# An FFT filter ahead of an expert layer: where the second stage puts one product, and what ScalarE does in which order there

## The chip, the cores and the metric

One core of one Trainium2 chip runs the whole program. The metric is the device time of one execution in microseconds (us); less is better. Five engines work side by side, each through its own queue in order: TensorE (PE in the profile; PEld are its weight loads), VectorE (DVE), ScalarE (ACT), GpSimd (POOL) and SyncE (SP), which only issues transfers here. An instruction that has to wait for a semaphore holds back all that stands behind it on its engine.

## What is computed

```python
h_filt = (np.maximum(pos_emb @ w1, 0.0) @ w2) * np.exp(-0.01 * pos)[:, None]
u = x * v                                     # 2 x 12480 x 128
Uf = np.fft.rfft(u, n=2 * S, axis=1)
Hf = np.fft.rfft(h_filt, n=2 * S, axis=0)
y = np.fft.irfft(Uf * Hf[None], n=2 * S, axis=1)[:, :S]
a = (x * y).reshape(24960, 128)
h = a @ moe_w_in                              # 128 -> 2048
g = np.maximum(h, 0.0) + moe_alpha * np.minimum(h, 0.0)
out = g @ moe_w_out                           # 2048 -> 128
```

A long convolution by way of a Fourier transform, a gate with `x`, and a two-layer network for every token. The kernel does the transforms as matrix products with tables, and the two weight matrices arrive as 64-bit words, whose two 32-bit halves the kernel itself turns into fp32 numbers.

## The kernel before

The transform is split in stages, and the 128 channels in two groups of 64 (`NG = 2`). For each group, stage 1 transforms over one index, stage 2 over the other and multiplies by the filter's spectrum, and stage 3 goes back along one index; after that, stage 4 and the expert layer (phase B) take most of the span. In the trace stage 2 runs twice: the **first run** stands at about 136 to 240 us, the **second run** at about 363 to 459 us, with stage 3 of the first group and stage 1 of the second group between them.

Stage 2 (`stage2`) goes over 90 frequencies, two at a time: 45 **pairs**, numbered 0 to 44 here. `skew` writes the code as a pipeline by hand: in each step every stage works on a pair of its own, and the order in which the stages stand in the call is the order of the instructions. What one step holds, with the engine:

- `low` (POOL, line 936) of the pair three back: the rest that is lost in the cast to fp16, two reads of SBUF.
- `high` (ACT, line 932) of the pair two back: the product's cast to fp16 into `z`.
- `total` of the pair one back: `real` (POOL, line 914) and `imaginary` (DVE, line 919), the real and the imaginary sum of the complex product; both read two tiles of SBUF.
- `transform` of this pair: 24 matmuls (PE, lines 881 to 886) into one of three PSUM buffers `mm`, then `hidden` (ACT, line 897), which copies the filter's two spectra out of PSUM into `hs`, and `product` (DVE, line 909): two multiplications of 512 elements, PSUM by SBUF into SBUF; `ta` is the data times the filter's real part, `tb` the data times its imaginary part.
- `neg` (ACT, line 848) for the pair two ahead: the negated sines that its matmuls read.
- `more`: one piece of a list of other work, below.
- `load` (SP, line 841): a table of 512 KB for every second pair, six steps ahead of its matmuls.

The last two pairs' products are not in this pipeline but in `end`, whose pieces a planner (`Plan`) orders together with the next stage; it keeps `product`, `real` and `imaginary` as they are.

In the first run the list of `more` is `weights_in`: the first weight matrix in four blocks of 512 columns. `read(n)` takes a block's words from its load in seven pieces, one in each step: an absolute value (ACT, line 595, into the PSUM bank `mb[1]`), four bit operations (DVE, lines 561, 564, 567 and 570; the last completes the fp32 numbers, and behind it SP issues the load of the next block, line 586, into the tile that it has just read), a square (ACT, line 600) and four matmuls with one column each (PE, line 601) into columns 0 to 15 of the PSUM bank `mb[0]`. `later(read, 6)` starts a block every six steps. Then come two pieces for a power-of-two scale, and `halves(n)`, started every three steps: four scaled diagonals (ACT, line 605), one matmul that needs them (PE, line 606, into `mb[1]`), a multiplication (DVE, line 607, SBUF by PSUM), a cast, a subtraction (POOL, line 609) and a store (SP, line 610). In the second run the list is short: `unscale` does six small operations on DVE (lines 1141 to 1147, one partition), and two steps later four matmuls with one column each (`turn`, line 1151) into `mb[0]`.

Of the kernel before, what the change touches and what calls it, by code (L numbers as in the profile page):

```python
# [104 lines left out]
def skew(items, *stages):  # L105

    n = len(items)
    for t in range(n + max(j for j, _ in stages)):
        for j, stage in stages:
            if 0 <= t - j < n:  # L110
                stage(items[t - j])
# [178 lines left out]
def body(ctx, tc, A, out, stop=None, dbg=None):  # L290
# [278 lines left out]
    def completed(out, t, lo):  # L569
        ve.scalar_tensor_tensor(out=out, in0=lo, scalar=29, in1=t, op0=ALU.logical_shift_right, op1=ALU.bitwise_or)  # L570

    def weights_in(mb, ru, du, pu, su):

        w = units(ru, 2).bitcast(I32)
        lo, hi = (w.rearrange("p (n w) -> p w n", w=2)[:, j] for j in range(2))
        t = mb[1].bitcast(I32)
        d = [units(u) for u in du]
        sq = units(su).bitcast(BF16)
        diag = [units(ru).bitcast(BF16)[:, j * 512:(j + 1) * 512].rearrange("p (f c) -> p f c", c=128) for j in range(2)]

        def four(x):
            return x.rearrange("p (f c) -> p f c", c=128)

        def load(n):
            if n < NFT // 4:
                sy.dma_start(out=w, in_=A["wi"][:, n * 512:(n + 1) * 512].bitcast(I32))

        def bound():
            load(0)
            ve.tensor_tensor(out=room_a, in0=keep, in1=keep, op=ALU.mult)  # L590
            ve.tensor_single_scalar(out=room_a, in_=room_a, scalar=1.0, op=ALU.max)

        def read(n):
            x = sq[:, n % 2 * 512:n % 2 * 512 + 512]
            yield lambda: ac.activation(mb[1], hi.bitcast(F32), AF.Abs)
            yield lambda: within(ve, mb[1])
            yield lambda: shifted(t, t)
            yield lambda: signed(t, hi)
            yield lambda: (completed(d[n].bitcast(I32), t, lo), load(n + 1))
            yield lambda: ac.activation(x, d[n], AF.Square)  # L600
            yield lambda: [te.matmul(mb[0][:, 4 * n + f:4 * n + f + 1], four(x)[:, f], ones[:, :1], start=True, stop=True) for f in range(4)]

        def halves(n):
            p, g = half(units(pu[n % 2])), diag[n % 2]
            yield lambda: [ac.activation(g[:, f], eye, AF.Copy, scale=pw[:, 4 * n + f:4 * n + f + 1]) for f in range(4)]
            yield lambda: te.matmul(mb[1], ones, g.rearrange("p f c -> p (f c)"), start=True, stop=True)
            yield lambda: ve.tensor_tensor(out=d[n], in0=d[n], in1=mb[1], op=ALU.mult)
            yield lambda: ac.activation(p[:, :, 0], four(d[n]), AF.Copy)
            yield lambda: po.tensor_tensor(out=p[:, :, 1], in0=four(d[n]), in1=p[:, :, 0], op=ALU.subtract)
            yield lambda: sy.dma_start(out=w_d[n], in_=p)  # L610

        def later(gen, s):
            parts = [list(gen(n)) for n in range(NFT // 4)]
            for x in range(s * (NFT // 4 - 1) + len(parts[0])):
                fs = [parts[n][x - s * n] for n in range(NFT // 4) if 0 <= x - s * n < len(parts[n])]
                yield lambda fs=fs: [f() for f in fs]

        yield bound
        yield none
        yield from later(read, 6)  # L620
        yield lambda: (ve.tensor_tensor(out=mb[0][:, 16:32], in0=mb[0][:, :16], in1=room_a, op=ALU.mult),
                       scales(mb[0][:, 32:48], mb[0][:, 16:32], pw, 192))
        yield lambda: inverse(ipw, pw)
        yield from later(halves, 3)

    def load_words(raws, n):
        sy.dma_start(out=raws[n].bitcast(I32), in_=A["wo"][:, n * 512:(n + 1) * 512].bitcast(I32).rearrange("p (u e) -> p u e", u=2))
# [54 lines left out]
    def phase_a():  # L682
# [167 lines left out]
        def stage2(tu, au, bu, hu, nu, extra, loaded=0):  # L850

            st = {}
            tws = {}

            def load(f0):
                if f0 % FB == 0:
# [10 lines left out]
            def transform(f0):  # L867
# [19 lines left out]
                st["p", f0] = p, *(units(u[x % n]).rearrange("p (a m) -> p a m", a=2) for u, n in ((hu, 2), (au, 4), (bu, 2)))  # L887
                if f0 < NF - 4:
                    hidden(f0)
                    product(f0)  # L890

            def hidden(f0, b0=0, b1=NB):

# [11 lines left out]
            def product(f0, b0=0, b1=NB):  # L905
                p, hs, ta, tb = st["p", f0]
                m = slice(b0 * 2 * ZC, b1 * 2 * ZC)
                for t, a in ((ta, 0), (tb, 1)):
                    ve.tensor_tensor(out=t[:, :, m], in0=p[:, :, m], in1=hs[:, a:a + 1, m].to_broadcast([128, 2, (b1 - b0) * 2 * ZC]), op=ALU.mult)  # L909

            def real(f0, b0=0, b1=NB, e=po):
                _, _, ta, tb = st["p", f0]
                m = slice(b0 * 2 * ZC, b1 * 2 * ZC)
                e.tensor_tensor(out=ta[:, 0, m], in0=ta[:, 0, m], in1=tb[:, 1, m], op=ALU.subtract)  # L914
# [4 lines left out]
                ve.tensor_tensor(out=ta[:, 1, m], in0=ta[:, 1, m], in1=tb[:, 0, m], op=ALU.add)  # L919

            def total(f0):
                real(f0)
                imaginary(f0)

            def place(f0, b0, b1):

# [14 lines left out]
            def until(last, stage):  # L941
                return lambda f0: stage(f0) if f0 <= last else None

            skew(list(range(0, NF, 2)), (9, until(NF - 10, low)), (8, until(NF - 8, high)), (7, until(NF - 6, total)),
                 (6, until(NF - 4, transform)), (4, neg), (4, more), (0, load))

            def end(P):

# [502 lines left out]
```

## Time and profile before

| | us |
|---|---|
| median of 3 runs | 1632.72 (1629.75 to 1633.54) |
| profiled execution | 1629.31 |
| its span, first to last instruction | 1627.5 |
| PE busy | 1549.3 (95% of the span) |
| DVE, ACT, POOL busy | 1288.0, 1329.6, 1036.1 |
| PE's granted clock, mean | 0.985 of 2.4 GHz |

The profiled execution has 1.8 us around its span. A matmul's record is longer than its distance from the next one, since matmuls are pipelined, so PE's busy time says little of how close PE is to its limit; the distance from start to start does. The same holds for a VectorE instruction: its record overlaps that of the next by some 0.08 us. Most of the span, from about 500 us on, is phase B, which the change leaves as it is.

### The profile page before, as it was taken

How to read it: one execution, taken by the hardware profiler on the slowest of the kernel's cores; microseconds unless marked ns; L12 is line 12 of the kernel's file. 1: busy time of each engine (PE TensorE's matmuls, PEld its weight loads, DVE VectorE, ACT ScalarE, POOL GpSimd, SP SyncE). 2: the span in 40 equal slices, each digit the busy share in tenths (PEclk: the TensorE clock that was granted, in tenths of full speed). 3: DMA queues.
4: the chain of work that ended last, by engine and by line, in shares of the span. 5: the costliest groups of instructions: out<-in, count | busy, mean ns of one | idle time of the engine just before them, and what ended most of it. 6: DMA issues, size and time to landing. Idle time of an engine off the chain costs nothing.

```text
span 1627.5 us, 34281 instructions
## 1 busy us (share of the span) xinstructions
PE 1549.3 (95%) x13452; PEld 1090.9 (67%) x13452; DVE 1288.0 (79%) x1867; ACT 1329.6 (82%) x2203; POOL 1036.1 (64%) x728
## 2 busy tenths in 40 slices
PE   6888888999988999999999999999999999999998
PEld 4778878889987566666666666665666666666664
DVE  7998988989987777777777777778777777777775
ACT  6887777887866888888888888888888888888886
POOL 6797896978963655556655566555565555665554
PEclk8999998999999999999999999999999999999999
DMA  6453437874358320202212021120202202022000
GB/s 200 138 155 130 157 133 207 250 222 153 130 159 237 96 56 25 57 21 57 62 35 57 21 57 49 49 57 21 57 30 68 57 21 57 21 77 57 20 11 20
DMA packets 91663, 141.86 MB, mean 87 GB/s; under 512 B 7057, under 2 KB 59891, under 8 KB 90061
## 3 DMA queue, kind: packets, MB, share of 16 engines
q1 hardware_dynamic: 90525, 139.10, 29.3%
q8 instruction: 105, 1.72, 0.4%
q10 hardware_dynamic: 976, 0.57, 0.1%
q14 instruction: 57, 0.47, 0.1%
HBM read 99.02 MB, written 40.63 MB: 86 GB/s over the span
## 4 chain that ended last, share of the span: by engine, by line
PE 72%; DVE 13%; POOL 4%; ACT 4%; issue 4%; DMA 3%; SPq 0%; POOLq 0%; ACTq 0%; DVEq 0%
PE hp L1273 31%; PE o L1273 31%; DVE ring L909 6%; DVE ring L919 3%; POOL ring L761 2%; DMA first<-in_xv 1%; PE yp L280 1%; PE yp L281 1%; PE yp L282 1%; PE mm L1010 1%; PE mm L1012 1%; POOL ring L752 1%; PE mm L1011 1%; DVE z L810 1%; POOL ring L724 1%
## 5 line engine op out<-in xcount | busy, mean ns | idle before, releaser
L1350 POOL TENSOR_TENSOR g_lo<-ring,g_hi 128x780 f16<-128x780 f32 x288 | 481.2, 1675 | 473.9 <-ACT g_hi L1349 473.9
L1343 DVE SCALAR_TENSOR_TENSOR ring<-ring,keep,hp 128x780 f32<-128x780 f32 x512 | 524.8, 1025 | 268.5 <-ACT ring L1342 259.2
L1342 ACT ACTIVATE ring<-hp 128x780 f32<-128x780 f32 x512 | 419.1, 819 | 162.2 <-PE hp L1273 161.0
L1273 PEld LDWEIGHTS <-w 128*128 128x128 f16 x3840 | 368.5, 97 | 269.5 <-issue 13.7
L1273 PE MATMUL hp<-ah,w 128*128 128x390 f16 x1984 | 489.1, 328 | 0.2 <-DVE ring L1343 0.2
L1349 ACT ACTIVATE g_hi<-ring 128x780 f16<-128x780 f32 x512 | 433.5, 847 | 1.1 <-DVE ring L1343 1.1
L1273 PE MATMUL o<-g_hi,ring 128*128 128x390 f16 x1536 | 378.3, 328 | 1.2 <-ACT ot L1364 1.0
L1273 PEld LDWEIGHTS <-ring 128*128 128x128 f16 x2304 | 223.2, 97 | 160.6 <-issue 2.1
L1273 PE MATMUL hp<-alo,w 128*128 128x390 f16 x992 | 244.6, 328 | 0.8 <-DVE alo L363 0.8
L1350 DVE TENSOR_TENSOR g_lo<-ring,g_hi 128x780 f16<-128x780 f32 x224 | 230.1, 1027 | 0.0
L1273 PE MATMUL o<-g_lo,ring 128*128 128x390 f16 x768 | 189.6, 328 | 0.6 <-POOL g_lo L1350 0.6
L1253 POOL TENSOR_TENSOR gl<-gt,gh 90x1024 f16<-90x1024 f32 x62 | 153.3, 2473 | 1.3 <-ACT gh L1252 1.3
L909 DVE TENSOR_TENSOR ring<-mm,ring 128x512 f32<-128x512 f32 (+2 forms) x188 | 115.9, 656 | 13.6 <-ACT ring L897 13.5
L1273 PE MATMUL o<-g_hi,w 128*128 128x390 f16 x512 | 126.2, 328 | 0.0
L1010 PE MATMUL mm<-t,z 128*128 128x128 f16 x512 | 104.5, 235 | 12.0 <-ACT z L932 7.9
L936 POOL TENSOR_TENSOR z<-ring,z 128x512 f16<-128x512 f32 x88 | 105.6, 1201 | 3.2 <-ACT z L932 3.1
L1012 PE MATMUL mm<-t,z 128*128 128x128 f16 x512 | 103.5, 233 | 0.3 <-DVE z L936 0.3
L1011 PE MATMUL mm<-t,z 128*128 128x128 f16 x512 | 103.6, 234 | 0.0
L914 POOL TENSOR_TENSOR ring<-ring 128x256 f32<-128x256 f32 (+1 forms) x90 | 77.2, 858 | 29.0 <-DVE ring L909 28.7
L795 PE MATMUL mm<-t,ring 98*128 98x180 f16 x320 | 79.6, 252 | 12.2 <-ACT ring L758 3.7
L807 ACT ACTIVATE z<-mm 128x720 f16<-128x720 f32 (+1 forms) x99 | 74.0, 755 | 19.8 <-PE mm L797 18.7
L810 DVE TENSOR_TENSOR z<-mm,z 128x720 f16<-128x720 f32 (+1 forms) x99 | 85.4, 876 | 5.8 <-ACT z L807 5.3
(214 smaller groups left out, 3126.5 us busy)
## 6 DMA issues: line engine op xcount, KB each, us to landing
gt<-g_d SPq DMA_DIRECT2D x16, 1440.0 KB
g_d<-ring SPq DMA_DIRECT2D x28, 720.0 KB
ring<-in_tw SPq DMA_DIRECT2D x34, 512.0 KB
ring<-in_xv SPq DMA_DIRECT2D x72, 196.0 KB
xt<-in_xt SPq DMA_DIRECT2D x31, 390.0 KB
out_t<-ot SPq DMA_DIRECT2D x31, 390.0 KB
first<-in_xv SPq DMA_DIRECT2D x56, 196.0 KB
first<-in_tw SPq DMA_DIRECT2D x12, 512.0 KB
```

Of the source, the lines that this page charges most:

```text
L810: ve.tensor_tensor(out=zb[:, 1, :, x:y, cs], in0=pv()[:, :, x:y], in1=zb[:, 0, :, x:y, cs], op=ALU.subtract)
L909: ve.tensor_tensor(out=t[:, :, m], in0=p[:, :, m], in1=hs[:, a:a + 1, m].to_broadcast([128, 2, (b1 - b0) * 2 * ZC]), op=ALU.mult)
L936: e.tensor_tensor(out=zl, in0=v, in1=zh, op=ALU.subtract)
L1010: te.matmul(o, hi, t3[:, 0], start=True, stop=False)
L1011: te.matmul(o, hi, t3[:, 1], start=False, stop=False)
L1012: te.matmul(o, lo, t3[:, 0], start=False, stop=True)
L1253: po.tensor_tensor(out=dl, in0=src, in1=dh, op=ALU.subtract)
L1273: te.matmul(o[:, b, :TOK], w, d[:, b], start=start and n == 0, stop=stop and n == 2)
L1342: ac.activation(neg, h, AF.Relu, scale=-1.0)
L1343: ve.scalar_tensor_tensor(out=acts[n], in0=neg, scalar=keep[:, f:f + 1], in1=h, op0=ALU.mult, op1=ALU.add)
L1349: ac.activation(gh, a, AF.Copy)
L1350: (po if n % 2 or n % NFT == 0 else ve).tensor_tensor(out=gl, in0=a, in1=gh, op=ALU.subtract)
```

## The change

Five edits, all around stage 2:

- `product` in the pipeline becomes `products`: `tb`'s half with the imaginary data first (256 elements), then `ta` as before (512), then the other cross product (256) last, and that one goes to `cross`, columns 256 to 511 of the PSUM bank `mb[0]`, not to `tb`.
- The imaginary sum in the pipeline takes `cross` from PSUM as its second operand (line 932 now).
- In the call of `skew`, `high` of the older pair stands behind `transform`; so ACT copies the filter's spectra first and casts the older pair behind that.
- The loads of blocks 1 to 3 of the words are issued by ACT behind the square, not by SP behind the last bit operation.
- `later(read, 7)` in place of 6, and `later(halves, 2)` in place of 3.

```diff
-                sy.dma_start(out=w, in_=A["wi"][:, n * 512:(n + 1) * 512].bitcast(I32))
+                (ac if n else sy).dma_start(out=w, in_=A["wi"][:, n * 512:(n + 1) * 512].bitcast(I32))
...
-            yield lambda: (completed(d[n].bitcast(I32), t, lo), load(n + 1))
-            yield lambda: ac.activation(x, d[n], AF.Square)
+            yield lambda: completed(d[n].bitcast(I32), t, lo)
+            yield lambda: (ac.activation(x, d[n], AF.Square), load(n + 1))
...
-        yield from later(read, 6)
+        yield from later(read, 7)
...
-        yield from later(halves, 3)
+        yield from later(halves, 2)
...
+            cross = mb[0][:, 2 * NU:4 * NU]
...
-                    product(f0)
+                    products(f0)
...
+            def products(f0):
+                p, hs, ta, tb = st["p", f0]
+                m = slice(0, 2 * NU)
+                ve.tensor_tensor(out=tb[:, 1], in0=p[:, 1, m], in1=hs[:, 1, m], op=ALU.mult)
+                ve.tensor_tensor(out=ta, in0=p[:, :, m], in1=hs[:, :1, m].to_broadcast([128, 2, 2 * NU]), op=ALU.mult)
+                ve.tensor_tensor(out=cross, in0=p[:, 0, m], in1=hs[:, 1, m], op=ALU.mult)
...
             def total(f0):
+                ta = st["p", f0][2]
                 real(f0)
-                imaginary(f0)
+                ve.tensor_tensor(out=ta[:, 1], in0=ta[:, 1], in1=cross, op=ALU.add)
...
-            skew(list(range(0, NF, 2)), (9, until(NF - 10, low)), (8, until(NF - 8, high)), (7, until(NF - 6, total)),
-                 (6, until(NF - 4, transform)), (4, neg), (4, more), (0, load))
+            skew(list(range(0, NF, 2)), (9, until(NF - 10, low)), (7, until(NF - 6, total)),
+                 (6, until(NF - 4, transform)), (8, until(NF - 8, high)), (4, neg), (4, more), (0, load))
```

How the instructions stand, at the three places that matter. First PE, first run, behind the 24 matmuls of pair 6, where block 0's one-column matmuls follow (`mb_100` is the bank `mb[0]`; in brackets the semaphores that an instruction waits for). Before:

```order
L885 LDWEIGHTS ring
L885 MATMUL mm_99<-z,ring 128x6x32
L886 LDWEIGHTS ring
L886 MATMUL mm_99<-z,ring 128x6x32
L601 LDWEIGHTS first [waits Activation_49]
L601 MATMUL mb_100<-ones,first 128x1
```

Now (the line 886 of before is 887):

```order
L886 LDWEIGHTS ring
L886 MATMUL mm_99<-z,ring 128x6x32
L887 LDWEIGHTS ring
L887 MATMUL mm_99<-z,ring 128x6x32
L601 LDWEIGHTS first [waits Activation_49]
L601 MATMUL mb_100<-ones,first 128x1 [waits DVE_49]
```

The place is the same; the first one-column matmul has a second wait. The count that it waits for is that of line 917, `cross`, of the same pair, in all four blocks (pairs 6, 13, 20 and 27; before, the matmuls stood behind pairs 6, 12, 18 and 24). The matmuls of `turn` behind pair 5 of the second run, which waited for line 1147, wait for `cross` of pair 5, which stands behind line 1147 on DVE. The imaginary sum behind such matmuls waits for PE.

DVE, first run, pairs 1 and 2 with the first two bit operations of block 0 (lines 561 and 564). Before:

```order
L909 TENSOR_TENSOR ring<-mm_98,ring 128x512 x2
L561 TENSOR_SCALAR mb_101<-mb_101 128x512
L919 TENSOR_TENSOR ring<-ring 128x256
L909 TENSOR_TENSOR ring<-mm_97,ring 128x512 x2
L564 TENSOR_SCALAR mb_101<-mb_101 128x512
L919 TENSOR_TENSOR ring<-ring 128x256
```

Now:

```order
L915 TENSOR_TENSOR ring<-mm_98,ring 128x256
L916 TENSOR_TENSOR ring<-mm_98,ring 128x512
L917 TENSOR_TENSOR mb_100<-mm_98,ring 128x256
L561 TENSOR_SCALAR mb_101<-mb_101 128x512
L932 TENSOR_TENSOR ring<-ring,mb_100 128x256
L915 TENSOR_TENSOR ring<-mm_97,ring 128x256
L916 TENSOR_TENSOR ring<-mm_97,ring 128x512
L917 TENSOR_TENSOR mb_100<-mm_97,ring 128x256
L564 TENSOR_SCALAR mb_101<-mb_101 128x512
L932 TENSOR_TENSOR ring<-ring,mb_100 128x256
```

The bit operations keep their place between a pair's products and its imaginary sum; a step has one instruction more.

ACT, first run, from pair 5 on, with the square of block 0 (line 600). Before:

```order
L932 ACTIVATE z<-ring 128x2x4x64
L897 ACTIVATE ring<-mm_97 128x512
L848 ACTIVATE ring<-ring 128x512
L600 ACTIVATE first<-ring 128x512
L932 ACTIVATE z<-ring 128x2x4x64
L897 ACTIVATE ring<-mm_99 128x512
L848 ACTIVATE ring<-ring 128x512
L595 ACTIVATE mb_101<-ring 128x512
```

Now:

```order
L898 ACTIVATE ring<-mm_97 128x512
L941 ACTIVATE z<-ring 128x2x4x64
L848 ACTIVATE ring<-ring 128x512
L600 ACTIVATE first<-ring 128x512
L586 DMA ring<-in_wi 128x1024
L898 ACTIVATE ring<-mm_99 128x512
L941 ACTIVATE z<-ring 128x2x4x64
L848 ACTIVATE ring<-ring 128x512
L898 ACTIVATE ring<-mm_98 128x512
L941 ACTIVATE z<-ring 128x2x4x64
L848 ACTIVATE ring<-ring 128x512
L595 ACTIVATE mb_101<-ring 128x512
```

The copy of the spectra (897, now 898) stands ahead of the cast (932, now 941), the next block's load is ACT's, and its absolute value (595) comes one pair later.

## Rows read from the trace of the kernel before

**Rows 1.** Busy time by stretch: PE, PEld, DVE, ACT, POOL; granted clock; DMA share, GB/s.

```profile
135.50:239.50 104.00, 93.02 (x1104) 89.52 (x1103) 92.27 (x161) 83.14 (x163) 89.29 (x88) 1.00 0.36 128
362.10:455.20 93.10, 91.24 (x1096) 90.38 (x1096) 87.52 (x143) 72.49 (x135) 83.28 (x85) 1.00 0.40 138
```

**Rows 2.** Timeline of DVE, first run: start, us, then the instruction; idle before it.

```profile
162.68 1.28 DVE L909 TENSOR_TENSOR ring<-mm,ring 128x512 f32<-128x512 f32 x2
163.88 0.67 DVE L570 SCALAR_TENSOR_TENSOR ring<-ring,mb 128x512 int32<-128x512 int32 x1
164.48 0.57 DVE L919 TENSOR_TENSOR ring<-ring 128x256 f32<-128x256 f32 x1
164.97 1.28 DVE L909 TENSOR_TENSOR ring<-mm,ring 128x512 f32<-128x512 f32 x2
166.28 0.43 DVE L919 TENSOR_TENSOR ring<-ring 128x256 f32<-128x256 f32 x1
166.62 1.28 DVE L909 TENSOR_TENSOR ring<-mm,ring 128x512 f32<-128x512 f32 x2
```

**Rows 3.** The same view of DVE, second run, one imaginary sum.

```profile
426.34 0.76 DVE L919 TENSOR_TENSOR ring<-ring 128x256 f32<-128x256 f32 x1
```

**Rows 4.** Timeline, first run: pair 0's last matmul and its first product.

```profile
138.75 0.25 PE L886 MATMUL mm<-z,ring 128*128 128x192 f16 x1
...
139.73 1.29 DVE L909 TENSOR_TENSOR ring<-mm,ring 128x512 f32<-128x512 f32 x2 [1.92 <-ACT ring L897]
```

**Rows 5.** Timeline of PE, first run, around two blocks' one-column matmuls.

```profile
163.91 0.25 PE L886 MATMUL mm<-z,ring 128*128 128x192 f16 x1
165.27 0.25 PE L601 MATMUL mb<-ones,first 128*128 128x1 bf16 x4 [1.11 <-ACT first L600]
165.38 0.24 PE L881 MATMUL mm<-z,ring 128*128 128x192 f16 x1
...
179.47 0.25 PE L601 MATMUL mb<-ones,first 128*128 128x1 bf16 x4 [1.11 <-ACT first L600]
```

**Rows 6.** Waits of PE in the first run: in total, times, longest.

```profile
PE mm L884 <- ACT ring L848: 2.7, 4, 0.7
```

**Rows 7.** Timeline of PE, first run, around one matmul of `halves`.

```profile
201.62 0.25 PE L886 MATMUL mm<-z,ring 128*128 128x192 f16 x1
...
202.94 0.24 PE L881 MATMUL mm<-z,ring 128*128 128x192 f16 x1
```

**Rows 8.** Timeline, first run's end: pair 42's products, pair 44's fourth matmul.

```profile
237.20 0.69 DVE L909 TENSOR_TENSOR ring<-mm,ring 128x512 f32<-128x512 f32 x1 [0.97 <-ACT ring L897]
...
237.67 0.26 PE L884 MATMUL mm<-z,ring 128*128 128x192 f16 x1 [0.59 <-ACT ring L848]
```

**Rows 9.** Timeline, second run: DVE's small chain, then PE around `turn`.

```profile
374.41 0.41 DVE L1141 TENSOR_SCALAR mb<-s_u 1x256 int32<-1x256 int32 x1
...
377.23 0.40 DVE L919 TENSOR_TENSOR ring<-ring 128x256 f32<-128x256 f32 x1
...
376.19 0.25 PE L886 MATMUL mm<-z,ring 128*128 128x192 f16 x1
377.36 0.60 PE L1151 MATMUL mb<-one,first 1*128 1x1 f32 x4 [0.92 <-DVE first L1147]
377.89 0.26 PE L881 MATMUL mm<-z,ring 128*128 128x192 f16 x1
```

**Rows 10.** Timeline, second run's end: pair 42's products, PE's last and next matmul.

```profile
452.92 1.28 DVE L909 TENSOR_TENSOR ring<-mm,ring 128x512 f32<-128x512 f32 x2
...
455.04 0.25 PE L886 MATMUL mm<-z,ring 128*128 128x192 f16 x1
459.16 0.34 PE L1010 MATMUL mm<-t,z 128*128 128x128 f16 x1 [3.87 <-ACT z L932]
```

**Rows 11.** Busy time by stretch behind that, columns as in rows 1.

```profile
457.74:464.56 6.82, 5.40 (x49) 5.23 (x50) 4.48 (x13) 2.69 (x9) 5.96 (x6) 0.50 0.83 220
```

**Rows 12.** Groups by line and form, first run: count, busy us, mean ns, idle before.

```profile
L607 DVE TENSOR_TENSOR ring<-ring,mb 128x512 f32<-128x512 f32 x4 | 2.7, 676 | 0.0
```

## The prediction

> **What bounds the kernel now.** I read the busy times by stretch first, then the timeline engine by engine inside the two runs of stage 2; the rest of the span isn't touched. In both runs PE, DVE and POOL are all busy nearly throughout and PE's clock is full [rows 1], so shares don't tell the bound; distances from start to start do. PE's own pace: in the second run 39 pairs lie between 377.89 and 455.04 + 0.08 [rows 9, 10], so 1.98 us a pair. DVE's pace: the two products take 0.60 each (162.68 to 163.88), a bit operation 0.60 (163.88 to 164.48), the imaginary sum 0.49 behind one (164.48 to 164.97): 2.29 for a step with a bit operation [rows 2]. Without one the sum starts 0.11 late, since it needs the product just ahead of it (two products from 164.97 end at 166.17, the sum starts at 166.28), and with POOL at work it lasts 0.76 in place of 0.43 [rows 2, 3]: 1.20 + 0.11 + 0.68 = 1.99. So the second run has DVE and PE level, and the first is DVE's wherever `read` adds to it. PE also stops by itself: 1.28 (163.99 to 165.27) for the square, some 0.7 four times for the negated sines, and 1.24 (201.70 to 202.94, its 0.22 of matmul within) four times in `halves` [rows 5 to 7]. One cycle of `read`, six pairs, takes 179.47 - 165.27 = 14.20, which is 2.37 a pair [rows 5].
>
> **The change, part by part.** I count from a pair's end, its last matmul's start + 0.08.
>
> *DVE's step.* A 256-element instruction takes 0.34 from start to start (166.28 to 166.62) where POOL doesn't hold it up [rows 2]. The new sum has one operand in PSUM; the nearest row is line 607, SBUF by PSUM, 676 ns four times [rows 12], as long as any 512-element product, so I take no hold-up (bounds: 0 and the 0.33 of rows 3). New step: 0.34 + 0.60 + 0.34 products, 0.11, 0.34 sum = 1.73; with a bit operation, which covers the 0.11, 2.22. The gain is 0.26 and 0.07 a step. A product that writes into PSUM has no row here; I take no difference to one that writes SBUF, and 0.05 a step either way for the range.
>
> *ACT's order and the load.* Products start 0.90 behind a pair's end when nothing is in the way (138.83 to 139.73) [rows 4], so copying the spectra first brings at most this 0.90 to each step. The load from ACT takes one issue from ACT, beside its waits, and frees SP's queue; block n + 1's absolute value is still two steps behind its load, now with PE's stop between them, so I expect the four waits for the sines (2.7 in all [rows 6]) to vanish. `halves` keeps its four stops of 1.24: the diagonals are still one step ahead of their matmul and still behind the copy, the cast and the negation on ACT.
>
> *The new wait.* PE's one-column matmuls wait for `cross` of the pair whose matmuls PE has just made. That can't be early: 0.90 to the products, then 0.34 + 0.60 + 0.43 until the last has its result, 0.05 back to PE: PE stops 2.32 even with an idle DVE, against 1.28 now. Behind it in PE's queue stands the next pair; for that pair ACT, then DVE wait in turn. What I know of the reason: in the trace `turn`, on this bank, waits for DVE [rows 9], but for data. The Trainium skill, page "PSUM — Partial Sum Buffer", section "PSUM bank collisions raise a hardware error", says to guard PSUM by bank and not by address, as two engines in one bank at once are an error; no run here shows one. By that rule sharing `mb[0]` between `cross` and the columns has this price; by addresses alone, which never overlap, the waits would be the old ones and the sum the rival "no stop" below.
>
> *First run.* Products of pair 0 at 139.73 as now, of pair 1 at 138.83 + 1.98 + 0.90 = 141.71. Four bit operations stand behind pairs 1 to 4: pair 5 at 141.71 + 4 x 2.22 = 150.59, pair 6 at 152.32, its `cross` done at 153.69, PE goes on at 153.74. PE had ended pair 6 at 150.71: a stop of 3.03. From there a cycle: four matmuls 0.11 [rows 5], pair 7's end at 2.09, its products 2.99, pair 8's 4.97, four steps of 2.22 to 13.85, 1.73 to 15.58, + 1.37 + 0.05 = 17.00 for seven pairs, 2.43 a pair against 2.37. The blocks' matmuls come at 153.74, 170.74, 187.74 and 204.74. Then 17 pairs from 204.85 at 1.98, and 4 x 1.24: pair 44 ends at 243.47. Now it ends at 237.67 + 1.73 = 239.40 [rows 8]. **+4.07**. With an idle DVE (stops of 2.32 + 0.11): 138.83 + 44 x 1.98 + 4 x 2.43 + 4.96 = 240.63, +1.2, the lower bound.
>
> *Second run, `turn`.* Products of pair 3 start at 373.21 (1.20 ahead of 374.41) and now end at 374.49; the six small operations take 2.82 (374.41 to 377.23) [rows 9]: 377.31. Sum 0.34, pair 4's step 1.73, pair 5's products 1.37, 0.05: PE goes on at 380.80, four matmuls 0.53, next pair at 381.33 in place of 377.89. **+3.44**. PE ended pair 5 at 376.27: a stop of 4.53 where it was 1.09. From there PE sets the pace at 1.98 in both kernels.
>
> *The ends.* Products of pair 42 start 2.20 ahead of pair 44's end in both runs (239.40 - 237.20, 455.12 - 452.92) [rows 8, 10]; unhindered they start 3.06 ahead. The last pairs' chain on DVE may so be 0.86 earlier against PE: **-0.86** in the second run, half of it in the first, whose following loads go by PE's last reads of the tables: **-0.43** (bounds 0 and -1.72 together).
>
> *PE's clock.* Now PE's stops of 1.28 leave it at 1.00 (2.4 GHz), and a stop of 4.04 (455.12 to 459.16) is followed by 0.50 (1.2 GHz) from 457.74 to 464.56, that is from 2.62 behind its start until 9.44 [rows 1, 10, 11]. `turn`'s 4.53 I take as that: half speed from 378.9 to 385.7, of which PE works from 380.80 on, 4.9, and does half as much: **+2.45**. The four stops of 3.03 lie between 1.28 and 4.04. If the clock falls, the pair behind the stop takes 3.96 for 1.98, and DVE has nothing else to do then: 0 to 1.98 each. I take half, 1.0: **+4.0**.
>
> Sum: 4.07 + 3.44 - 0.86 - 0.43 + 2.45 + 4.0 = **+12.7** on the profiled execution's 1629.3: 1642.0. The median of the runs lies 3.4 above that execution, and the same sum on it gives 1645.4; I keep 1642.0 and let the range reach over both.
>
> **Rivals.**
> - *The clock stays.* The stops are there, but PE doesn't fall to half: +12.7 - 6.45 = +6.2, **1635.5**. For it: stops of 1.28 cost nothing [rows 1, 5]. Against: 4.53 is longer than the 4.04 that did.
> - *No stop* (the other side). PE's matmuls into `mb[0]` come through as early as now, because `cross` is done when PE gets there; stops of 1.28 + 0.11 at most. First run: 138.83 + 87.12 + 4 x 1.39 + 4.96 = 236.47, -2.9; ends -1.3: -4.2, **1625.1**. It decides from a stop of some 1.5 us on. For it: DVE gains 0.07 to 0.26 a step and the sines' stops go. Against: `cross` reads what PE has only just written, and the shortest way is 2.32.
> - *The port stays.* POOL still holds up the sum. Steps of 2.37 and 2.08: a cycle of 18.05, +4.2 for four; second run 37 pairs x 0.10 = 3.7: +20.6, **1650**. For it: the sum still reads one tile of SBUF while POOL reads two. Against: line 607 doesn't show it [rows 12].
> - *The stage between swallows the first run's delay*, as it has transfers to wait for: 3.44 - 0.86 + 2.45 = +5.0, **1634.3**. Against: its loads overwrite tables that PE reads last, so they start later too.
>
> **How the numbers follow.** Forecast 0.55, clock stays 0.20, no stop 0.10, swallowed 0.08, port 0.07. About 0.2%, some 3.3 us, is what a measurement can tell from no change. The forecast, most of "clock stays" and half of "swallowed" lie above that; with my step times 0.1 off, the small sums fall within it: slower 0.78, within 0.13, faster 0.09. The range: below, the lower bound of the first run (+1.2), `turn` without a fall of the clock (+3.44) and the ends (-1.72) give 1632.2, left half out: 1633. Above, every stop with the full 1.98 and the ends at 0: 4.07 + 3.44 + 2.45 + 7.9 = 17.9 on 1629.3 is 1647.2, on the median 1650.6: 1650.
>
> **What would show it.** In the changed profile: the imaginary sum at 0.42 to 0.43 us each time, not 0.57 to 0.76; four stops of PE ahead of the one-column matmuls, about 3 us each, put down to DVE; one stop of 4.5 us at `turn`; no more waits of line 884's kind for the sines; stretches at 0.50 behind `turn` and behind one or more of the four. I'm wrong if PE's stops at the one-column matmuls are under 1.5 us, if the sum stays above 0.5 us, or if pair 44 of the first run ends before 239.4.

## The result: 1644.31 us, and where it went

The changed kernel takes 1644.31 us (median of 5 runs, 1642.02 to 1647.35) against 1632.72 before (1629.75 to 1637.69): a ratio of 1.0069, interval 1.0055 to 1.0083, so 11.6 us slower, at least 9.0. The forecast was 1642.0 in 1633 to 1650. The profiled execution is the longest of the five, 1647.35 with a span of 1645.6. It reaches stage 2 later than that of before (140.26 against 135.96), and stage 2 itself explains what the medians show, so I compare the two runs of stage 2 by their own length: from the last matmul of pair 0 to the last matmul of pair 44, read in PE's timeline.

| | first run | second run | both, against before |
|---|---|---|---|
| before | 100.58 | 88.75 | |
| changed | 106.50 | 95.12 | +12.3 |

Busy time by stretch, columns as in [rows 1]: the two runs, then the two stretches in them in which PE's clock is down.

```profile
139.80:249.70 109.90, 93.78 (x1103) 91.65 (x1102) 88.31 (x205) 82.05 (x164) 81.60 (x89) 0.98 0.36 120
376.80:475.30 98.50, 93.20 (x1086) 92.19 (x1084) 81.04 (x184) 73.01 (x136) 78.31 (x86) 0.97 0.39 127
158.40:161.80 3.40, 3.40 (x24) 3.21 (x23) 0.19 (x1) 0.03 (x1) 0.00 (x0) 0.51 0.02 6
393.90:400.70 6.80, 6.18 (x37) 5.88 (x38) 1.42 (x5) 1.13 (x3) 1.10 (x2) 0.50 0.01 2
```

Where [rows 1] had DVE busy for 92 of 104 us in the first run and 88 of 93 in the second, it is now 88 of 110 and 81 of 99: DVE has less to do, and it waits. PE's timeline shows for what, at the first and the second block's one-column matmuls and at `turn`; these rows answer to [rows 5] and [rows 9]:

```profile
154.93 0.25 PE L887 MATMUL mm<-z,ring 128*128 128x192 f16 x1
157.89 0.24 PE L601 MATMUL mb<-ones,first 128*128 128x1 bf16 x4 [2.71 <-DVE mb L917]
157.99 0.24 PE L882 MATMUL mm<-z,ring 128*128 128x192 f16 x1
...
173.42 0.25 PE L887 MATMUL mm<-z,ring 128*128 128x192 f16 x1
176.46 0.24 PE L601 MATMUL mb<-ones,first 128*128 128x1 bf16 x4 [2.80 <-DVE mb L917]
...
389.91 0.25 PE L887 MATMUL mm<-z,ring 128*128 128x192 f16 x1
394.52 1.01 PE L1160 MATMUL mb<-one,first 1*128 1x1 f32 x4 [4.36 <-DVE mb L917]
395.46 0.34 PE L882 MATMUL mm<-z,ring 128*128 128x192 f16 x1
```

And the waits of PE in the first run, in total, times, longest (in [rows 6] the sines stood here with 2.7; they are gone):

```profile
PE mb L601 <- DVE mb L917: 11.3, 4, 2.9
PE mb L606 <- ACT ring L605: 3.8, 4, 1.0
```

What ends these waits is now line 917, `cross`, where it was ScalarE's square in [rows 5]. DVE's timeline ahead of the first of these stops shows the shape of a step, one with a bit operation and two without:

```profile
152.56 0.42 DVE L915 TENSOR_TENSOR ring<-mm,ring 128x256 f32<-128x256 f32 x1
152.90 0.68 DVE L916 TENSOR_TENSOR ring<-mm,ring 128x512 f32<-128x512 f32 x1
153.50 0.42 DVE L917 TENSOR_TENSOR mb<-mm,ring 128x256 f32<-128x256 f32 x1
153.83 0.68 DVE L570 SCALAR_TENSOR_TENSOR ring<-ring,mb 128x512 int32<-128x512 int32 x1
154.42 0.41 DVE L932 TENSOR_TENSOR ring<-ring,mb 128x256 f32<-128x256 f32 x1
154.75 0.42 DVE L915 TENSOR_TENSOR ring<-mm,ring 128x256 f32<-128x256 f32 x1
...
156.48 0.42 DVE L915 TENSOR_TENSOR ring<-mm,ring 128x256 f32<-128x256 f32 x1
156.82 0.68 DVE L916 TENSOR_TENSOR ring<-mm,ring 128x512 f32<-128x512 f32 x1
157.41 0.42 DVE L917 TENSOR_TENSOR mb<-mm,ring 128x256 f32<-128x256 f32 x1
158.17 0.42 DVE L932 TENSOR_TENSOR ring<-ring,mb 128x256 f32<-128x256 f32 x1 [0.33 <-PE mb L601]
```

A step is 152.56 to 154.75, 2.19, or 154.75 to 156.48, 1.73. `cross` of pair 6 starts at 157.41 and PE goes on at 157.89, 0.48 later; the sum behind it (line 932) waits for PE in turn. The sum's mean over the first run is 417 ns, where [rows 2, 3] had up to 760.

### The profile page after: what moved, and what is told of

Same layout as the page of the kernel before. It is cut to its first block, busy times and chain, and to the rows that moved or that the text cites. A ratio compares the mean times of both kernels' runs of the same rounds, so it can differ in the third digit from the quotient of the medians.

```text
span 1645.6 us, 34372 instructions
## 1 busy us (share of the span) xinstructions
PE 1560.1 (95%) x13452; PEld 1102.1 (67%) x13452; DVE 1279.5 (78%) x1953; ACT 1328.1 (81%) x2203; POOL 1021.2 (62%) x728
## 4 chain that ended last, share of the span: by engine, by line
PE 82%; DVE 7%; DMA 4%; ACT 3%; issue 2%; POOL 2%; SPq 0%; POOLq 0%; ACTq 0%; DVEq 0%
PE hp L1282 31%; PE o L1282 31%; PE mm L1019 2%; PE mm L882 1%; PE mm L883 1%; PE mm L884 1%; PE mm L1021 1%; PE mm L885 1%; PE mm L886 1%; PE mm L887 1%; PE mm L1020 1%; PE yp L280 1%; PE yp L281 1%; PE yp L282 1%; DMA first<-in_xv 1%
## 5 line engine op out<-in xcount | busy, mean ns | idle before, releaser
L945 POOL TENSOR_TENSOR z<-ring,z 128x512 f16<-128x512 f32 x88 | 101.7, 1156 | 34.5 <-ACT z L941 28.6
L1019 PE MATMUL mm<-t,z 128*128 128x128 f16 x512 | 103.7, 234 | 11.6 <-ACT z L941 8.7
L898 ACT ACTIVATE ring<-mm 128x512 f32<-128x512 f32 x86 | 51.2, 595 | 51.0 <-ACT ring L848 22.6
L795 PE MATMUL mm<-t,ring 98*128 98x180 f16 x320 | 81.0, 256 | 11.1 <-DVE z L810 2.8
L797 PE MATMUL mm<-t,ring 98*128 98x180 f16 x320 | 80.9, 256 | 7.4 <-POOL ring L761 7.3
```

Source lines behind the costliest of these rows:

```text
L795: te.matmul(o, data(c, 0), t1[:, 0], start=True, stop=False)
L945: e.tensor_tensor(out=zl, in0=v, in1=zh, op=ALU.subtract)
L1019: te.matmul(o, hi, t3[:, 0], start=True, stop=False)
```

## The experiments

**Theory:** `cross` and the one-column matmuls share the bank `mb[0]`; PE waits, four times in the first run and once at `turn`, for a product that can't be early. **Rivals:** the loss comes from the new order on ScalarE, from the words' loads and steps, or from writing a product to PSUM at all.

Every kernel was timed beside the kernel before on the same chip. The lengths are those of the table above, the ratios and intervals are to before.

| kernel | first run | second run | both, against before | ratio | interval |
|---|---|---|---|---|---|
| changed, again | 108.04 | 95.08 | +13.8 | 1.0069 | 1.0055 to 1.0084 |
| cross_only | 110.22 | 94.21 | +15.1 | 1.0061 | 1.0037 to 1.0085 |
| columns_late | 106.45 | 94.97 | +12.1 | 1.0060 | 1.0037 to 1.0082 |
| in_sbuf | 106.51 | 89.55 | +6.7 | 1.0051 | 1.0034 to 1.0068 |
| turn_bank | 106.59 | 89.08 | +6.3 | 1.0038 | 1.0021 to 1.0055 |
| order_only | 101.49 | 89.00 | +1.2 | 0.9995 | 0.9979 to 1.0010 |
| spread | 96.72 | 89.40 | -3.2 | 0.9978 | 0.9965 to 0.9991 |
| own_buffer | 96.34 | 88.86 | -4.1 | 0.9973 | 0.9958 to 0.9987 |
| own_first_bank | 96.31 | 88.86 | -4.2 | 0.9970 | 0.9959 to 0.9981 |
| combined | 95.50 | 89.28 | -4.6 | 0.9969 | 0.9956 to 0.9982 |
| words_only | 97.80 | 89.78 | -1.8 | 0.9966 | 0.9953 to 0.9980 |

For nearly all of them the two runs of stage 2 give the time: +6.3 us is 0.38% of 1633, as measured for turn_bank; -4.1 is 0.25%, measured 0.27% for own_buffer. The exceptions are cross_only and words_only. cross_only's +15.1 would be 0.92%, more than the 0.85% that its interval allows: its profiled execution is the longest of its six, 1652.73 against a median of 1645.99. words_only stands below.

### The product in another place of PSUM

```diff
-                ve.tensor_tensor(out=cross, in0=p[:, 0, m], in1=hs[:, 1, m], op=ALU.mult)
+                ve.tensor_tensor(out=p[:, 1, 2 * NU:4 * NU], in0=p[:, 0, m], in1=hs[:, 1, m], op=ALU.mult)
...
-                ve.tensor_tensor(out=ta[:, 1], in0=ta[:, 1], in1=cross, op=ALU.add)
+                ve.tensor_tensor(out=ta[:, 1], in0=ta[:, 1], in1=p[:, 1, 2 * NU:4 * NU], op=ALU.add)
```

> The changed kernel with one thing moved: the last cross product goes to unused and already copied columns of the pair's own PSUM buffer mm (columns 256 to 511 of its second bank), not to the bank mb[0] that the one-column matmuls use. If the sharing of mb[0] is the cause, the waits of PE for line 917 are gone: at the four one-column matmuls PE waits at most some 1.3 us, for ScalarE's square, at the turn 1.1 us for DVE's small chain; from pair 0's end to pair 44's end the first run takes about 97.6 us (106.50 in the changed kernel, 100.58 before), the second about 88.2 (95.12 and 88.75); the time is 1624 to 1629. If instead a product written to PSUM, or the new order on ScalarE and of the words, costs the time, stops or longer steps stay and the time is 1638 to 1645.

PE's timeline of that kernel at the second block:

```profile
168.71 0.25 PE L886 MATMUL mm<-z,ring 128*128 128x192 f16 x1
169.47 0.25 PE L601 MATMUL mb<-ones,first 128*128 128x1 bf16 x4 [0.51 <-ACT first L600]
169.58 0.24 PE L881 MATMUL mm<-z,ring 128*128 128x192 f16 x1
```

The stop of 3.0 is one of 0.76, and ScalarE's square is again what ends it. The product is still written to PSUM, made last, with the new orders and loads around it, and the kernel is now faster than before the change: 1629.27 us, 0.3 above the range that I expected (the second run is 0.7 longer than I had put it, the first 1.3 shorter). All three rivals keep what they blame here, and none costs what was lost. So the shared bank is the cause, and its price is the distance to the changed kernel, falls of PE's clock included: 106.50 + 95.12 - 96.34 - 88.86 = 16.4 us. Against before, the rest of the change is a gain of 4 to 5 us.

### The product in SBUF

```diff
-                ve.tensor_tensor(out=cross, in0=p[:, 0, m], in1=hs[:, 1, m], op=ALU.mult)
+                ve.tensor_tensor(out=tb[:, 0], in0=p[:, 0, m], in1=hs[:, 1, m], op=ALU.mult)
...
-                ve.tensor_tensor(out=ta[:, 1], in0=ta[:, 1], in1=cross, op=ALU.add)
+                ve.tensor_tensor(out=ta[:, 1], in0=ta[:, 1], in1=tb[:, 0], op=ALU.add)
```

> The changed kernel with the last cross product written to SBUF (tb's real half, as before the change), still made last and in the new order. Shared bank as the cause: no wait of PE for it, so no stop of 3 us. What is lost against the version in the pair's own PSUM buffer is what the sum pays for two SBUF operands beside POOL: sums of 0.5 to 0.76 us in place of 0.42, a step of about 2.0 us in place of 1.73, so DVE is level with PE; first run 99 to 101 us from pair 0's to pair 44's end, time 1627 to 1633. If the operand in PSUM gives nothing, it is as fast as the version in the own buffer.

This missed: 1641.77 us, with no wait of PE for the last product in it. The first run's sums as a group, then timelines of POOL and of DVE:

```profile
L931 DVE TENSOR_TENSOR ring<-ring 128x256 f32<-128x256 f32 x43 | 34.9, 811 | 0.7
```

```profile
185.27 1.16 POOL L944 TENSOR_TENSOR z<-ring,z 128x512 f16<-128x512 f32 x1
...
184.75 0.68 DVE L567 SCALAR_TENSOR_TENSOR mb<-ring,mb 128x512 int32<-128x512 int32 x1
185.35 1.37 DVE L931 TENSOR_TENSOR ring<-ring 128x256 f32<-128x256 f32 x1
186.64 0.41 DVE L914 TENSOR_TENSOR ring<-mm,ring 128x256 f32<-128x256 f32 x1
```

POOL's subtraction, two reads of SBUF, runs from 185.27 to 186.43. The sum that starts 0.08 behind it ends at 186.72, 0.29 after POOL; undisturbed it takes 0.41. I had taken the sum's cost from before, 0.5 to 0.76, but how long it is held up depends on where in POOL's instruction it falls. In the profiles of before and of in_sbuf, 150 sums of 256 elements start inside a POOL instruction with more than 0.15 us of it left, and 149 of them end 0.27 to 0.29 behind POOL's end. The other one starts 0.01 behind POOL's start: it takes 0.41, and POOL's subtraction takes 1.44 in place of 1.16. In in_sbuf, 11 of the first run's 43 sums fall at the start of a subtraction and last 1.22 to 1.37. The Trainium skill, page "SBUF — State Buffer", section "SBUF: two separate sides", says that a DVE instruction with two SBUF inputs and a GpSimd instruction that reads SBUF take a shared port pair as an exclusive lock, whichever starts first, for the whole instruction; these ends agree. The first run has one fall of PE's clock in it as well (0.50 from 172.5 to 175.8, behind a stop of 2.51). So the operand in PSUM is worth 106.51 + 89.55 - 96.34 - 88.86 = 10.9 us beside the new orders: a large gain that the shared bank took away, and more.

### Turn's result in the other bank

```diff
-                te.matmul(mb[0][:, b:b + 1], iv[:, b, :], one1, start=True, stop=True)
+                te.matmul(mb[1][:, 384 + b:385 + b], iv[:, b, :], one1, start=True, stop=True)
...
-lambda: ve.tensor_copy(scal, mb[0][:, :B])
+lambda: ve.tensor_copy(scal, mb[1][:, 384:384 + B])
```

> The changed kernel with the four matmuls of turn in the other bank, mb[1], columns 384 and 385, and the copy of their result read from there. Shared bank: the stop at turn falls from 4.61 to 1.1 us, the half clock behind it goes, the second run falls from 95.12 to about 88.5 us between the ends of pairs 0 and 44; the four stops of about 3.0 us in the first run stay; 1644.3 - 6.5 = about 1638. If turn waits for its data and not for the bank, nothing changes: 1644.

1639.53 us, 1.5 above what I expected, with the four stops where they were. In the second run PE's wait there reads:

```profile
PE mb L1160 <- DVE first L1156: 1.0, 1, 1.0
```

It waits for its data, as line 1151 did before [rows 9]. The second run is 6.0 us shorter than the changed kernel's, the first as long as there: against before, the change's loss is two parts of nearly equal size, 5.9 in the first run and 6.4 in the second.

### The columns one step later

```diff
+            yield none
             yield lambda: [te.matmul(mb[0][:, 4 * n + f:4 * n + f + 1], four(x)[:, f], ones[:, :1], start=True, stop=True) for f in range(4)]
```

> The changed kernel with the one-column matmuls one step later than the square they need (an empty step between), so that they stand behind pairs 7, 14, 21 and 28. Shared bank: each waits for the cross product of its own new pair, which DVE reaches one step of 1.73 against PE's 1.98 less late, so the stops are 2.8 us in place of 3.05 and the time is 1641 to 1645. If they wait for the square, as before the change, the four stops fall under 0.5 us and the time is about 1632.

1642.77 us, as expected. The square is long done, and PE still stops (these lines have one number more in this kernel):

```profile
172.34 0.25 PE L888 MATMUL mm<-z,ring 128*128 128x192 f16 x1
175.12 0.24 PE L602 MATMUL mb<-ones,first 128*128 128x1 bf16 x4 [2.53 <-DVE mb L918]
```

The stop is 2.78 here and 2.71 to 2.83 at the four, where it was 2.96 to 3.19: one step of 1.98 - 1.73 = 0.25 less late, or a little more. Waiting longer doesn't help, since every later pair brings a `cross` of its own.

### One part at a time

Each starts from the kernel before. cross_only takes `products` and the sum from `cross` of the change:

```diff
-                    product(f0)
+                    products(f0)
...
-                imaginary(f0)
+                ve.tensor_tensor(out=ta[:, 1], in0=ta[:, 1], in1=cross, op=ALU.add)
```

> The kernel before with the products alone: the imaginary data's product first, the last cross product into mb[0], the sum from there; ScalarE's order, the words' loads and steps as before. Shared bank: four stops of 3 us or more put down to the cross product, the turn's stop at 4.5 to 4.7; first run 104 to 108 us, second about 95; time 9 to 13 above before, nearly all of the change's loss. If the loss needs the new orders: within 3 of before.

order_only takes the order of the stages:

```diff
-            skew(list(range(0, NF, 2)), (9, until(NF - 10, low)), (8, until(NF - 8, high)), (7, until(NF - 6, total)),
-                 (6, until(NF - 4, transform)), (4, neg), (4, more), (0, load))
+            skew(list(range(0, NF, 2)), (9, until(NF - 10, low)), (7, until(NF - 6, total)),
+                 (6, until(NF - 4, transform)), (8, until(NF - 8, high)), (4, neg), (4, more), (0, load))
```

> The kernel before with the changed order on ScalarE alone: the copy of the spectra ahead of the older pair's cast. If that order is what puts VectorE's sum under GpSimd's subtraction (as in the version with the product in SBUF, whose sums took up to 1.37 us), sums average 0.7 to 0.85 us here (0.61 before), the first run takes 102 to 107 us from pair 0's to pair 44's end (100.58 before), and the time is 2 to 7 above before. If the earlier copy is a gain by itself, or neutral, the sums stay at 0.6 and the time is 0 to 4 below before.

words_only takes the loads and the steps:

```diff
-            yield lambda: (completed(d[n].bitcast(I32), t, lo), load(n + 1))
-            yield lambda: ac.activation(x, d[n], AF.Square)
+            yield lambda: completed(d[n].bitcast(I32), t, lo)
+            yield lambda: (ac.activation(x, d[n], AF.Square), load(n + 1))
...
-        yield from later(read, 6)
+        yield from later(read, 7)
...
-        yield from later(halves, 3)
+        yield from later(halves, 2)
```

> The kernel before with the words' part alone: loads of blocks 1 to 3 from ScalarE behind the square, blocks 7 steps apart, halves 2 apart. By my steps the four waits for the negated sines (2.7 us) go, and DVE's seven steps of a block, 4 x 2.29 + 3 x 1.99 = 15.13, fit PE's 13.86 + 1.28: 98 to 99.5 us from pair 0's to pair 44's end in the first run, second run unchanged at 88.75, time 1 to 3 below before. If ScalarE's issue costs more than SP's: at or above before.

cross_only carries the loss alone: 11.0 us by its medians (1645.99 against 1634.96), and 10.9 us of waits for line 917 in the first run. That run is 2.2 longer than the upper end of what I expected, with PE at half clock behind each of the four stops; the stop at `turn`, 4.33, is a little shorter than I expected. Busy time by stretch, columns as in [rows 1]:

```profile
157.10:160.50 3.40, 2.90 (x22) 2.75 (x22) 0.87 (x3) 1.18 (x2) 2.10 (x3) 0.50 0.83 331
174.20:177.60 3.40, 3.40 (x24) 3.13 (x22) 0.39 (x1) 1.18 (x2) 1.34 (x2) 0.50 0.56 223
191.20:194.60 3.40, 3.40 (x25) 3.13 (x23) 0.00 (x0) 1.56 (x4) 1.15 (x1) 0.51 0.44 172
208.30:211.70 3.40, 3.40 (x24) 3.21 (x22) 1.18 (x3) 1.63 (x3) 0.23 (x2) 0.50 0.28 59
```

order_only missed the 2 to 7 us: no difference in time. Its sums last 644 ns in the first run (613 before), so copying first does put them a little more under POOL; neither this order nor the words' part (608) comes near the 811 of in_sbuf, which has the products' order besides. That order with a sum from SBUF was not run alone. words_only is a gain, and a larger one than the 1 to 3 us that I expected: 97.80 in the first run, and the waits for the sines fall to 1.0 in total, not to none. By its ratio it gains 3.3 to 7.7 us, more than stage 2 shows in its profile (-1.8, with 1.0 lost at the second run's start). The profiled execution is the longest of its twelve (1635.82, median 1629.78); where the rest of the gain lies I didn't settle. Nor do the three parts add up by their ratios: they make 10.0 - 0.8 - 5.6 = +3.6 us of 1633, the whole change 11.3; by stage 2's lengths they make 15.1 + 1.2 - 1.8 = +14.5, near the whole change's +12.3 and +13.8.

### Attempts at a faster version

All three keep the product in the pair's own buffer. combined, against own_buffer, has an empty step ahead of the one-column matmuls (as in columns_late), of the diagonals' matmul and of `turn`:

```diff
+            yield none
             yield lambda: te.matmul(mb[1], ones, g.rearrange("p f c -> p (f c)"), start=True, stop=True)
...
-            yield lambda: po.tensor_tensor(out=p[:, :, 1], in0=four(d[n]), in1=p[:, :, 0], op=ALU.subtract)
-            yield lambda: sy.dma_start(out=w_d[n], in_=p)
+            yield lambda: (po.tensor_tensor(out=p[:, :, 1], in0=four(d[n]), in1=p[:, :, 0], op=ALU.subtract), sy.dma_start(out=w_d[n], in_=p))
...
-(lambda: (exponents(), both(), rest()), lambda: None, turn,
+(lambda: (exponents(), both(), rest()), lambda: None, lambda: None, turn,
```

> The changed kernel with the cross product in the pair's own PSUM buffer and three of PE's waits moved one step from what they wait for: the one-column matmuls behind the square, the diagonals' matmuls behind the diagonals, the turn behind its small chain; the last two pieces of halves share a step, so that the list still fits. From the version in the own buffer, 1629.3: the stops of 1.0 and 1.2 us, four each, and the turn's 1.1 go, 4 x 1.0 + 4 x 1.2 + 1.1 = 9.9: about 1619.5, 1617 to 1623. If DVE then sets the pace in the first run, the stops turn into longer steps elsewhere and the time stays above 1625.

own_first_bank, against own_buffer, makes the 512-element product first and writes `cross` into the buffer's first bank:

```diff
+                ve.tensor_tensor(out=ta, in0=p[:, :, m], in1=hs[:, :1, m].to_broadcast([128, 2, 2 * NU]), op=ALU.mult)
                 ve.tensor_tensor(out=tb[:, 1], in0=p[:, 1, m], in1=hs[:, 1, m], op=ALU.mult)
-                ve.tensor_tensor(out=ta, in0=p[:, :, m], in1=hs[:, :1, m].to_broadcast([128, 2, 2 * NU]), op=ALU.mult)
-                ve.tensor_tensor(out=p[:, 1, 2 * NU:4 * NU], in0=p[:, 0, m], in1=hs[:, 1, m], op=ALU.mult)
+                ve.tensor_tensor(out=p[:, 0, 2 * NU:4 * NU], in0=p[:, 0, m], in1=hs[:, 1, m], op=ALU.mult)
```

> The version in the pair's own buffer with the 512-element product made first and the cross product written to the first bank of the buffer, which only the product two instructions back and itself read. In the version before this one the cross product started 0.71 us behind the 512-element product in place of 0.60, as it waits for that one's last read. Here that 0.11 goes in every step; DVE's seven steps of a block are 4 x 2.22 + 3 x 1.73 = 14.07 in place of 14.87, first run 96.34 to 93 to 95.5 us from pair 0's to pair 44's end, second run unchanged; 1 to 3 us less than the version in the own buffer. If DVE's pace isn't what sets the first run there, no change.

spread, against own_first_bank, has the empty step ahead of the one-column matmuls, and:

```diff
-(lambda: (exponents(), both(), rest()), lambda: None, turn,
+(exponents, lambda: (both(), rest()), lambda: None, turn,
```

> The one above with the one-column matmuls one step behind the square and the turn's small chain on DVE split over two steps. If DVE's pace is out of the way, the four stops for the square (0.76 each) and the turn's (1.1) go: first run 91 to 93.5 us, second 87.3 to 88.2, 3 to 5 us less than the one above. If DVE still sets the pace, the waits come back as waits for a free PSUM buffer, as in the combined version.

None is clearly faster than own_buffer, so the gain that each expectation names first was missed. In combined and spread the other case came, in which DVE sets the pace; in own_first_bank the 0.11 did not go. DVE's timeline of own_buffer, then of own_first_bank:

```profile
399.15 0.68 DVE L915 TENSOR_TENSOR ring<-mm,ring 128x512 f32<-128x512 f32 x1
399.86 0.43 DVE L916 TENSOR_TENSOR mm<-mm,ring 128x256 f32<-128x256 f32 x1
400.33 0.42 DVE L931 TENSOR_TENSOR ring<-ring,mm 128x256 f32<-128x256 f32 x1
```

```profile
399.84 0.69 DVE L914 TENSOR_TENSOR ring<-mm,ring 128x512 f32<-128x512 f32 x1
400.45 0.41 DVE L915 TENSOR_TENSOR ring<-mm,ring 128x256 f32<-128x256 f32 x1
400.90 0.43 DVE L916 TENSOR_TENSOR mm<-mm,ring 128x256 f32<-128x256 f32 x1
401.36 0.42 DVE L931 TENSOR_TENSOR ring<-ring,mm 128x256 f32<-128x256 f32 x1
```

The 0.11 that `cross` (line 916 here) pays stays: 0.71 behind the 512-element product there, 0.45 behind the 256-element one here (0.34 without a wait). In own_first_bank the product just ahead reads the buffer's second bank and `cross` writes the first, and still the program makes it wait for that product (the count that it waits for is that of line 915 of the same pair, and it starts 0.04 behind that one's end, 400.86): these waits follow the whole tile, two banks, and not the bank or the columns. In combined the removed waits of PE came back as others, in PE's timeline behind `turn`'s chain and in the waits of the first run:

```profile
380.60 0.24 PE L882 MATMUL mm<-z,ring 128*128 128x192 f16 x1 [1.36 <-DVE ring L932]
```

```profile
PE mb L608 <- DVE ring L609: 3.4, 3, 1.5
```

Line 932 there is the sum that frees the pair's buffer. With `cross` in the pair's buffer DVE's steps are 2.32 and 1.86, 0.13 longer than the changed kernel's, so seven of them are 4 x 2.32 + 3 x 1.86 = 14.86, and a block's period is just that: 14.88 in own_buffer (153.83 to 168.71), 14.82 in combined, 14.84 in spread. The stop for the square had only shown that PE was ahead of DVE. The diagonals' matmul, made a step later, met the multiplication of the block ahead, which reads `mb[1]`.

### The changed kernel again

No edit; it is the changed kernel, run and profiled once more.

> The changed kernel once more, for a second profile: the four stops of 2.96 to 3.19 us and the turn's 4.61 at the same lengths to 0.1; what differs is where the granted clock falls: behind none to four of the four stops (one in the first profile), and behind the turn's always. Time 1642 to 1646.

1645.48 us; the stops are 2.96, 3.03, 3.20 and 3.13, at `turn` 4.61. The clock fell behind the first two of the four and stayed at 1.00 behind the others; the first three:

```profile
156.50:159.90 3.40, 3.40 (x24) 3.21 (x22) 1.06 (x3) 1.76 (x4) 0.57 (x1) 0.50 0.21 48
173.50:176.90 3.40, 3.23 (x24) 3.06 (x24) 0.54 (x2) 0.00 (x0) 0.65 (x1) 0.51 0.28 113
190.60:194.00 3.40, 1.72 (x24) 1.72 (x24) 2.05 (x5) 0.51 (x1) 2.16 (x3) 1.00 0.39 137
```

## Why the prediction was right, and where its sum was not

- **DVE's step**: 1.73 and 2.22 forecast, 1.73 and 2.19 measured; the sum at 0.42 each time. The rival in which POOL still holds it up is out for the sum with an operand in PSUM, and in_sbuf shows what it would have been.
- **The new wait**: from `cross` to PE 0.43 + 0.05 forecast, 0.48 measured. Stops from a pair's end of 3.03 forecast, 2.88 (157.89 - 155.01), 2.96, 3.11 and 3.06 measured; a cycle of 17.00, 16.92 and 17.06 (173.42 to 190.34 to 207.40). The rival "no stop" is out; own_buffer, where PE stops 0.76 and not for `cross`, has the gain that it named: 4.8 below before on the same chip, against its -4.2.
- **First run**: +4.07 forecast without the clock, +5.92 measured with it. Behind the first stop pairs 7 and 8 took 6.38 + 2.21, behind the second, at full clock, the same two took 5.04 + 1.98: the clock cost 1.57. The four stops of `halves` are 1.20 + 0.22 - 0.08 = 1.34 each, +0.4 in all against the 1.24 of the sum. They did not grow: the one in [rows 7] is the shortest of four, 1.10 from start to start where the others were 1.22, 1.21 and 1.21 before, and PE's wait for line 605 is 3.8 in total in both profiles. I had taken it for all four.
- **`turn`**: a stop of 4.53 forecast, 394.52 - 389.99 = 4.53 measured, and half clock from 393.9 to 400.7, 6.8 us long as forecast, from 3.9 us behind the stop's start on and not from 2.6, so that PE worked 6.2 us of it (from 394.5 on) in place of 4.9. Together +5.89 forecast, +6.37 measured in the second run.
- **The four falls of the clock** were the term with the wrong size: 4.0 forecast as half of 7.9, 1.57 in the profile, which had one fall. The changed kernel's second profile had two, cross_only four, columns_late two and turn_bank one: ten behind twenty stops of 2.71 to 3.20 from start to start. A stop of 2.71 had one and a stop of 3.19 had none, so their length doesn't decide it alone. Half of the stops was thus the right share over these profiles, but a fall cost 1.3 to 1.6 by the comparison above, not 1.98, which would make about 2.9, an estimate, for four stops. I don't know which of the executions without a profile had how many.
- **The ends**: -0.86 forecast for the second run, nothing measured; the first run's -0.43 can't be told from the spread of the stage behind it (last point). From the second run's last matmul to the next stage's first it takes 4.09 (475.13 to 479.22) where [rows 10] has 4.12. The step that failed is that an earlier DVE stays earlier. The chain that ends there, in order of time, changed then before:

```profile
474.87 0.87 DVE ring L922
475.74 1.11 DVE ring L927
476.85 0.56 DVE ring L910 x2
```

```profile
455.46 0.22 DVE ring L914
455.69 1.09 DVE ring L919
456.78 0.57 DVE ring L909 x2
```

The small sums of the end read two tiles of SBUF in both kernels, as `real` and `imaginary` weren't changed. Against PE's last matmul DVE gets to them 0.68 earlier (474.87 - 475.13 against 455.46 - 455.04), the first lasts 0.87 in place of 0.22, the second 1.1 in both, and the lead is gone. POOL makes two subtractions (line 945) there, which end at 475.66 and 476.77, and the two sums end 0.08 and 0.09 behind them; before, the first sum started 0.08 ahead of the first subtraction. That POOL holds them up fits these ends; I did not try it.

- **The sines' waits** went, as forecast: 2.7 to none on PE.
- **What the sum got right by balance**, which is luck: of the differences the four falls are -2.4, the ends +1.3, `halves` +0.4 and `turn` +0.5, which nearly cancel: 12.7 forecast, 12.3 in stage 2's two runs, 11.6 in the medians. The rivals "the clock stays" (+6.2) and "swallowed" (+5.0) lie below the interval's 9.0.
- **The reason of the wait**: I left open whether it goes by bank or by address. own_first_bank shows that in this program a wait can go by the tile, there between two products of DVE and across two banks; `mb[0]` is a tile of one bank, so the changed kernel can't tell tile from bank. The rule of the Trainium skill's page "PSUM — Partial Sum Buffer", section "PSUM bank collisions raise a hardware error", guards one bank against two engines: it asks for PE's wait on `mb[0]`, but not for the one in own_first_bank. No run here shows what happens without either.
- The stage between the runs took 124.2 us before and 127.7 in the changed profile, but 123.8 to 130.9 over all the profiles here, 124.0 in the changed kernel's second one; nothing here rests on it.

## What to carry to other kernels

A scratch place in PSUM that is free by its columns can still tie two engines together, by the waits that the program puts in: before sharing a tile, list who else writes and reads it, and what each must then wait for, the latest write in program order and not the one whose data it needs. An operand in PSUM freed DVE's sum from GpSimd here (0.40 to 0.42 us each time), and that was worth 10.9 us in a place that PE didn't have to share. And before removing a wait of the engine that is ahead, compute the period of the engine behind it: here DVE's seven steps were the block's period, and PE's waits only moved.

## What the runs showed of the hardware that I had not expected

- A DVE sum of 256 elements with two SBUF operands took 0.40 to 1.37 us, by how much was left of the GpSimd instruction in which it started: 149 of 150 ended 0.27 to 0.29 behind it. With one operand in PSUM it took 0.40 to 0.42 every time.
- A product that writes PSUM took no longer than one that writes SBUF: 0.41 to 0.43 for 256 elements in both cases.
- Stops of PE of 2.71 to 3.20 us in the first run were followed by a granted clock of 0.50 (1.2 GHz) ten times out of twenty, over five profiles, and a stop of 2.5 once out of two in in_sbuf; stops of up to 1.7 in the first run never.
